# A transformer block on one core: w1 loaded in parts of 6, 4 and 4 blocks, other loads behind pair 1's LayerNorm, and set places for the transposes of pairs 2 and 3

## The chip, the core and the metric

The kernel runs on one core of a Trainium2 chip. The core has a matrix engine (PE, whose weight loads have a row of their own, PEld), a vector engine (DVE), a scalar engine for activations (ACT), a general engine (POOL) and an engine that mainly issues DMAs (SP). Each engine runs its own instruction list in order and waits on semaphores for the others. Sixteen DMA engines move data between the chip's memory (HBM) and the core's on-chip memory. The metric is the device time of one execution, in microseconds (us); lower is better.

## The reference, cut to what matters

The input x is 2048 rows of 448 numbers in bf16. It is normalized once, and two branches read the result; both are added to x.

```python
xn = _layernorm(x, axis=-1)                       # (x - m) / sqrt(v + eps), no gain, no bias
# branch A: linear attention, 16 heads of 28
q, k, v = split(xn @ wqkv)                        # wqkv 448 x 1344
pq = einsum("bhsd,hdf->bhsf", q, w_phi); pk = einsum("bhsd,hdf->bhsf", k, w_phi)
phi_q = concat([softmax(pq), softmax(-pq)]); phi_k = concat([softmax(pk), softmax(-pk)])
kv = einsum("bhsf,bhsd->bhfd", phi_k, v); z = einsum("bhsf->bhf", phi_k)
o = einsum("bhqf,bhfd->bhqd", phi_q, kv) / (einsum("bhqf,bhf->bhq", phi_q, z)[..., None] + 1e-6)
# branch B: feed-forward
h = silu(xn @ w1)                                 # w1 448 x 1792
return x + o @ wo + h @ w2                        # w2 1792 x 448
```

## The kernel before, in words

The 2048 rows are 16 tiles of 128 rows, and two tiles make a pair (pairs 0 to 7). The 1792 columns of w1 are 14 blocks of 128 columns. The 448 rows of w1 are three slabs of 128 rows and a rest of 64 rows, which the kernel calls the tail. PE works with two halves of its rows at once (rows 0 to 63, `UP`, and 64 to 127, `LO`), so that every step is two matmuls of 64 rows side by side.

**Stages.** First the feed-forward branch's first product (FFN1, `xn @ w1`) runs for all pairs, while LayerNorm produces the next pairs. Then come the attention projections with their exponentials, then the attention output and the second product pair by pair. The change touches the FFN1 stage alone, its first 30 us above all.

**Loads (lines 543 to 604).** `load_x(t0, t1)` fetches tiles of x. `load_k` fetches columns of the three full slabs of w1: `w1a` blocks 0 to 3, `w1b` blocks 4 to 7, `w1c` blocks 8 to 13. `load_tail` fetches the 64 tail rows, once for each half (`w1t`, 224 KB each). For pairs 0 and 1 the tail comes instead from small early copies, `w1z`, which `load_z` fetches in a borrowed buffer (`EqT`): blocks 0 to 3 and 4 to 7 on ACT's queue, 8 to 13 on SP's. All other loads are issued by SP, in the order of the program. From `first_loads` on each load is also tied to come after the one before it. Four of these later loads are paced: `for o, d in zip(paced, evp): o.deps.add(d.id)` (line 1136) makes x of tiles 8 to 11, wqk, x of tiles 12 to 15 and wv wait for the ends of the LayerNorm of pairs 1, 2, 3 and 4.

**LayerNorm.** For each tile DVE takes `bn_stats` and `bn_aggr` (lines 608, 610); for each pair it adds eps (`ve`, 616), POOL raises to the power -1/2 (`rstd`, 617), and DVE writes the normalized rows (`xn`, line 624; pairs 0 and 1: line 646). PE transposes them (`xnT_tr`, by `trs`, whose instructions are on line 459) into PSUM banks 6 and 7, and DVE or ACT copies the result to `xnT` (`xnT_ev`; ACT for pair 2, DVE for pairs 3 and up). `lnz_first`, `lnz_second` and `ln_pair(p)` do this for pair 0, pair 1 and the pairs from 2 on.

**FFN1 for pairs 0 and 1.** `ffn1_single(p, f0, f1, i0, i1, bank)` takes the blocks f0 to f1 of one pair: the first half of the range on the upper rows, the second half on the lower, and of these halves the blocks i0 to i1. It makes two groups of steps: in the first group the rows and halves go straight (4 steps for each block pair: three slabs and the tail), in the second crossed (3 steps). A pair is so 49 steps of 256 columns. The calls for one pair are

```python
((0, 4, 0, 2), (4, 8, 0, 2), (8, FT, 0, 2), (8, FT, 2, 3))      # FT = 14
```

Calls are interleaved two by two: first group of u, first group of v, second group of u, second group of v. This is `order0`, and it is an order written out by hand, as order-only ties between PE instructions.

**FFN1 for pairs 2 to 7.** `ffn1_chunk` takes two pairs at once, two blocks at a time; it reads the tail from `w1t`. Between its units lie `fold_tr` (transposes of wqkv in the same banks 6 and 7 that LayerNorm's transposes use) and `fold`.

**The planner.** All other places are chosen by a list scheduler (`schedule`, line 218): it estimates durations and DMA arrivals, and gives each engine the instruction that can start first, with program order deciding between those that are ready within 60 ns. Ties in `odeps` are pure order on one engine; `deps` are real waits. The transposes of pairs 1 to 7 (but not of pair 0) are placed by it, and so is DVE's whole order. What it decides becomes the fixed order of each engine's list, whatever the chip then does.

Of the kernel before, what the change touches and what calls it, by code (L numbers as in the profile page):

```python
# [332 lines left out]
def bass_parallel_sum__linear_kernel_hedgehog__dense_activation_silu__prompt_kernel(  # L333
# [10 lines left out]
    S, D, H, DH, FF = 2048, 448, 16, 28, 1792  # L344
    NT, NPAIR = S // 128, S // 256
    KF = 3
    FT = FF // 128
# [7 lines left out]
    with es:  # L355
# [64 lines left out]
        P = _Prog()  # L420
# [122 lines left out]
        def load_x(t0, t1, eng="sp"):  # L543
            return load(x_sb[:, t0:t1, :], xt[:, t0:t1, :], (t1 - t0) * 128 * D * 2, f"x{t0}", eng)

        def load_k(dst, src, c0, c1, name, eng="sp", o=0):
            return load(dst[:, 0:KF, c0 - o:c1 - o], src[0:384, c0:c1].rearrange("(k p) f -> p k f", p=128),
                        384 * (c1 - c0) * 2, name, eng)

        def load_tail(dst, src, c0, c1, name, eng="sp", eng2="sp", o=0):  # L550
            return [load(dst[r, KF, c0 - o:c1 - o], src[384:448, c0:c1], 64 * (c1 - c0) * 2, name, e)
                    for r, e in ((UP, eng), (LO, eng2))]
# [9 lines left out]
        def load_z(f0, f1, eng):  # L562

            h = (f1 - f0) // 2
            o = w1z_no[0]
            w1z_no[0] += h * 128
            for j in range(2):
                for i in range(h):
                    w1z_at[f0 + j * h + i] = o + 128 * i
            return [load(w1z[r, o:o + h * 128], B_w1[384:448, (f0 + j * h) * 128:(f0 + j * h + h) * 128], 64 * h * 256, "w1z", eng)  # L570
                    for j, r in enumerate((UP, LO))]

        for o in load_z(0, 4, "act") + load_z(4, 8, "act"):
            o.odeps.add(pre_op.id)
        load_x(0, 1)
        load_k(w1_sb, B_w1, 0, 512, "w1a")
        load_x(2, 4)
        load_k(w1_sb, B_w1, 512, 1024, "w1b")
        load_z(8, 14, "sp")
        load_k(w1_sb, B_w1, 1024, FF, "w1c")  # L580
        load_x(4, 6)
        load_x(6, 8)
        load_tail(w1_sb, B_w1, 0, FF, "w1t")
        first_loads = len(P.ops)
        paced = []
        paced.append(load_x(8, 12))
        paced.append(load_k(wraw, A_wqkv, 0, 2 * D, "wqk"))
        load_tail(wraw, A_wqkv, 0, 2 * D, "wqkt")
        phi4 = A_w_phi.rearrange("(g a) d f -> a d g f", a=4)
        for hl in range(2):  # L590
            for r0, a in ((8, 2 + hl), (64, hl)):
                load(BD[r0 + DH * hl:r0 + DH * hl + DH, 0:4, DH * hl:DH * hl + DH], phi4[a], DH * 4 * DH * 2, "phi")
            load(BD[DH * hl:DH * hl + DH, 4, DH * hl:DH * hl + DH], A_w_phi[hl], DH * DH * 2, "phi0")
        paced.append(load_x(12, 16))
        paced.append(load_k(wv_sb, A_wqkv, 2 * D, 3 * D, "wv", "sp", 2 * D))
        load_tail(wv_sb, A_wqkv, 2 * D, 3 * D, "wvt", "sp", "sp", 2 * D)
        w2v = B_w2.rearrange("(f p) d -> p f d", p=128)
# [71 lines left out]
        def lnz_rest():  # L669

            a, b = xnT[LO, 3, 0:2, :], xnT[LO, 7, 0:2, :]
            P.dma(lambda e: e.dma_start(out=a, in_=b), 64 * 512, reads=[b], writes=[a], name="xnTt").odeps.add(paced[3].id)

        def lnz_first():

# [30 lines left out]
        def ln_pair(p, one_by_one=False):  # L706
            t0, t1 = 2 * p, 2 * p + 1
            for t in (t0, t1):
                ln_stats(t)
                if one_by_one:  # L710
                    ln_rstd(t, t + 1)
            if not one_by_one:
                ln_rstd(t0, t1 + 1)
            ln_norm(p, t0)
            ln_norm(p, t1)
            ln_tr(p, [0, 1, 2, 3, 4, 5, 6], 2 if p == NPAIR - 1 else 6, "act" if p in LN_ACT else "dve")
# [7 lines left out]
        def ffn1_chunk(p0, npair, f0, fend, units=(0, 2, 4)):  # L724
            n = npair * 128
            F = 512 // n
            while f0 < fend:
                f1 = min(fend, f0 + F)
                b0 = units[unit_no[0] % len(units)]
                unit_no[0] += 1  # L730
                jobs = []
                for ft in range(f0, f1):
                    jobs.append((lambda r, b: xnT[r, b, p0:p0 + npair, :].rearrange("p a c -> p (a c)"),
                                 lambda r, k, ft=ft: w1_sb[r, k, ft * 128:ft * 128 + 128],
                                 [banks[b0 + par][:, (ft - f0) * n:(ft - f0) * n + n] for par in range(2)],
                                 ft == f0, True))
                units_done.append(contract(jobs, n, True, True, "ffn1_mm"))
                w = f1 - f0
                src = psum[:, b0 * 512:(b0 + 2) * 512].rearrange("p (r c) -> p r c", r=2)[:, :, 0:w * n]
                if w == 1:  # L740
                    dst = hT[:, f0, :, p0:p0 + npair, :].rearrange("p r a c -> p r (a c)")
                else:
                    src = src.rearrange("p r (f c) -> p r f c", f=w)
                    dst = hT[:, f0:f1, :, p0:p0 + npair, :].rearrange("p f r a c -> p r f (a c)")
                o = act(dst, src, ACTF.Silu, "silu", table="silu")
                if exps:
                    o.odeps.update(exps)
                silus.append(o)
                f0 = f1

        def ffn1_single(p, f0, f1, i0, i1, b0, by_tile=False):

            h = (f1 - f0) // 2
            done = [[], []]
            for q, t0, t1 in (((0, 0, 1), (0, 1, 2), (1, 0, 2)) if by_tile else ((0, 0, 2), (1, 0, 2))):
                rr = (UP, LO) if q == 0 else (LO, UP)
                for k in range(KF + 1 - q):
                    for i in range(i0, i1):
                        parts = []
                        for j in range(2):  # L760
                            r, ft = rr[j], f0 + j * h + i
                            xx = xnT[r, k + 4 * t0:k + 4 * t1 - 3:4, p, :]
                            c = (i - i0) * 256 + t0 * 128
                            parts.append((banks[b0 + j][:, c:c + 128 * (t1 - t0)].rearrange("p (t c) -> p t c", c=128),
                                          w1z[r, w1z_at[ft]:w1z_at[ft] + 128] if k == KF else w1_sb[r, k, ft * 128:ft * 128 + 128], xx,
                                          q == 0 and k == 0 and i == i0 and t0 == 0, q == 1 and k == KF - 1))
                        done[q].append(mms(parts, "ffn1_mm", 132.0 / 2 if t1 - t0 == 1 else d_mm(256)))
            for o in done[1]:
                o.syncs.add(done[0][-1].id)
            src = psum[:, b0 * 512:(b0 + 2) * 512].rearrange("p (j f) -> p j f", j=2)[:, :, 0:256 * (i1 - i0)]  # L770
            dst = hT[:, f0:f1, :, p, :].rearrange("p (j i) r c -> p j i r c", j=2)[:, :, i0:i1]
            dst = dst.rearrange("p j i r c -> p j (i r) c")
            src = src.rearrange("p j (a c) -> p j a c", c=128)
            silus.append(act(dst, src, ACTF.Silu, "silu", table="silu"))
            return done
# [40 lines left out]

        ev0, order0 = lnz_first()
        banks_ = iter((0, 2, 4, 0, 2, 4, 0, 2))
        evp, passes = [], []
        for p in range(2):  # L820
            for f0, f1, i0, i1 in ((0, 4, 0, 2), (4, 8, 0, 2), (8, FT, 0, 2), (8, FT, 2, 3)):
                if p == 1 and f0 in (0, 4):
                    k = len(P.ops)
                    ln_pair(2 + f0 // 4)
                    evp.append(P.ops[-1])
                    for o in P.ops[k:]:
                        if o.eng == "dve":
                            o.odeps.add(last1)
                passes.append(ffn1_single(p, f0, f1, i0, i1, next(banks_), f0 == 0 and p == 0))
                if p == 0 and f0 == 0:  # L830
                    k = len(P.ops)
                    evp.append(lnz_second(1))
                    for o in P.ops[k:]:
                        if o.eng == "dve":
                            o.odeps.add(ev0.id)
                    last1 = [o.id for o in P.ops if o.eng == "dve"][-1]
        for u, v in zip(passes[0::2], passes[1::2]):
            order0 += [u[0], v[0], u[1], v[1]]
        for a, c in zip(order0, order0[1:]):
            for o in c:  # L840
                o.odeps.add(a[-1].id)
        ln_pair(4)
        evp.append(P.ops[-1])
        unit_no[0] = 0
        ffn1_chunk(2, 2, 0, 4, (4, 0, 2))
        ln_pair(5)
        for i in range(3):
            ffn1_chunk(2, 2, 4 + 2 * i, 6 + 2 * i, (4, 0, 2))
            fold_tr(3 * i)
# [283 lines left out]
        for a, c in zip(chain, chain[1:]):  # L1133
            for o in c:
                o.odeps.add(a[-1].id)
        for o, d in zip(paced, evp):
            o.deps.add(d.id)
        eks = [o.id for o in P.ops if o.name == "exp_k"]
        for o, d in zip(w2_loads + [wo_load], eks[0::2]):
# [2 lines left out]
        ops = P.ops  # L1142
# [109 lines left out]
```

## Time and profile before

| what | value |
|---|---|
| time of the kernel, median of 3 runs | 157.28 us (157.26 to 157.56) |
| the profiled execution's own time | 158.61 us |
| its span, first to last instruction | 156.8 us |
| PE busy | 149.9 us, 96% of the span |
| PEld, DVE, ACT, POOL busy | 98.0, 99.7, 76.0, 55.0 us |
| granted PE clock | 1.00 throughout |
| bytes moved by DMA | 9.60 MB |

The span is what the profile shows instruction by instruction; the execution's time has some 1.8 us around it. The kernel's chain of waits goes through PE for 80% of the span. A microsecond in which PE stands still early in the kernel is therefore worth looking for, and the rows of PE's weight loads (PEld) show such stops with the name of what ended them.

### The profile page before, as it was taken

To read this page: it belongs to the slowest core of one execution; us is meant where nothing else is said; L and a number is where in the kernel's file an instruction comes from. 1 tells how busy PE (TensorE), PEld (TensorE's weight loads), DVE (VectorE), ACT (ScalarE), POOL (GpSimd) and SP (SyncE) were. 2 spreads that over 40 slices of the span, in tenths; PEclk is the share of its full clock that TensorE was granted. 3 is DMA by queue.
4 is the path that set the end of the run, shared out by engine and by line. 5 is a ranking of instruction groups with operands and counts; after the bars stand their busy time and mean duration, and the time that the engine had idled before them with its cause. 6 is when DMAs were issued, how large, how long until landed. Compare 5 with 4: busy or idle time off the path is not lost.

```text
span 156.8 us, 5661 instructions
## 1 busy us (share of the span) xinstructions
PE 149.9 (96%) x2576; PEld 98.0 (62%) x2576; DVE 99.7 (64%) x177; ACT 76.0 (48%) x89; POOL 55.0 (35%) x79
## 2 busy tenths in 40 slices
PE   6988998999999899999999999999999999999993
PEld 4576886888964445445468887646565655555572
DVE  1948884974236889497696387793846657483203
ACT  3656765558859886986869755220201202021000
POOL 7111111120100677938678023534325160605000
PEclk9999999999999999999999999999999999999999
DMA  4995376000002532040000000001011010101012
GB/s 138 317 281 147 101 212 182 4 4 4 0 4 46 171 112 83 7 117 0 4 0 4 4 0 6 4 0 63 0 59 45 18 63 0 63 2 59 4 63 59
DMA packets 8628, 9.60 MB, mean 61 GB/s; under 512 B 1500, under 2 KB 8220, under 8 KB 8604
## 3 DMA queue, kind: packets, MB, share of 16 engines
q1 hardware_dynamic: 8140, 8.99, 19.3%
q8 instruction: 20, 0.33, 0.9%
q10 hardware_dynamic: 464, 0.25, 0.5%
q14 instruction: 4, 0.03, 0.1%
HBM read 7.37 MB, written 1.84 MB: 59 GB/s over the span
## 4 chain that ended last, share of the span: by engine, by line
PE 80%; DMA 8%; DVE 3%; ACT 3%; SPq 2%; issue 1%; POOL 1%; ACTq 0%
PE psum L446 77%; DMA x_sb<-in_A_x_dram 8%; PE psum L459 3%; SPq L538 2%; ACT EqT L465 1%; DVE st L608 1%; POOL rstd L617 1%; ACT L465 1%; DVE xnT L469 1%; DVE xn_sb L624 1%; ACT scr L465 1%; DVE mv L610 0%; DVE out_sb L1070 0%; DVE ve L616 0%; PE psum L957 0%
## 5 line engine op out<-in xcount | busy, mean ns | idle before, releaser
L446 PE MATMUL psum<-xnT,w_sb 64*128 64x256 bf16 (+1 forms) x768 | 47.4, 268 | 0.7 <-DMA w_sb<-in_B_w_dram 0.5
L446 PE MATMUL psum<-w_sb,hT 64*128 64x448 bf16 (+2 forms) x504 | 46.6, 328 | 0.0
L446 PEld LDWEIGHTS psum<-xnT,w_sb 64*128 64x128 bf16 x768 | 34.6, 94 | 6.6 <-DMA w_sb<-in_B_w_dram 1.0
L465 ACT ACTIVATE hT<-psum 128x1024 bf16<-128x1024 f32 (+1 forms) x29 | 28.3, 994 | 15.0 <-PE psum L446 12.2
L1041 POOL TENSOR_TENSOR xn_sb<-wraw 128x448 bf16<-128x448 f32 (+4 forms) x39 | 20.7, 563 | 36.9 <-DVE wraw L1019 36.9
L446 PEld LDWEIGHTS psum<-w_sb,hT 64*128 64x128 bf16 x504 | 22.7, 94 | 16.5 <-ACT oT L465 0.4
L465 ACT ACTIVATE oT<-psum 128x896 bf16<-128x896 bf16 x8 | 7.3, 917 | 40.4 <-PE psum L459 40.4
L890 POOL TENSOR_TENSOR scr<-scr,Rk 128x1792 bf16<-128x1792 bf16 x6 | 19.3, 3213 | 18.1 <-ACT scr L465 11.4
L465 ACT ACTIVATE EqT<-psum 128x1024 bf16<-128x1024 f32 x16 | 15.5, 1023 | 5.5 <-PE psum L446 5.5
L1019 DVE TENSOR_TENSOR wraw<-psum,Gq 128x1792 f32<-128x1792 f32 (+1 forms) x9 | 16.4, 1818 | 0.9
L446 PE MATMUL psum<-xnT,wqk_sb 64*128 64x512 bf16 x112 | 14.8, 378 | 0.4 <-ACT EqT L465 0.4
L1070 DVE TENSOR_TENSOR out_sb<-psum,x_sb 128x896 bf16<-128x896 f32 (+2 forms) x9 | 8.8, 981 | 9.5 <-PE psum L446 9.4
L1006 DVE RECIPROCAL R<-psum 128x64 f32<-128x64 f32 (+1 forms) x9 | 4.6, 512 | 14.9 <-PE psum L446 14.9
L446 PE MATMUL psum<-wv_sb,xnT 64*128 64x448 bf16 x112 | 14.0, 349 | 0.0
L617 POOL TENSOR_TENSOR rstd<-ve,neghalf 128x2 f32<-128x2 f32 (+1 forms) x8 | 5.4, 672 | 23.8 <-DVE ve L616 23.8
L608 DVE BATCH_NORM_STATS2 st<-x_sb 128x6 f32<-128x448 bf16 x16 | 9.8, 613 | 5.9 <-DMA x_sb<-in_A_x_dram 5.9
L446 PE MATMUL psum<-wo_sb,oT 64*128 64x448 bf16 (+2 forms) x126 | 13.6, 328 | 0.0
L446 PE MATMUL psum<-wqk_sb,xnT 64*128 64x448 bf16 x112 | 13.2, 349 | 0.0
L882 DVE TENSOR_REDUCE Sk<-scr 128x64 f32<-128x1792 bf16 x6 | 12.1, 2013 | 0.6 <-ACT scr L465 0.6
L469 DVE CAST scr<-psum 128x896 bf16<-128x896 f32 x6 | 6.5, 1084 | 9.1 <-PE psum L446 9.1
L465 ACT ACTIVATE scr<-psum 128x896 bf16<-128x896 f32 x12 | 10.4, 921 | 0.7 <-PE psum L446 0.4
L446 PEld LDWEIGHTS psum<-xnT,wqk_sb 64*128 64x128 bf16 x112 | 4.7, 94 | 6.9 <-PE psum L446 1.7
(69 smaller groups left out, 138.7 us busy)
## 6 DMA issues: line engine op xcount, KB each, us to landing
out_dram<-out_sb SPq DMA_DIRECT2D x7, 224.0 KB, 1.9
w_sb<-in_B_w_dram SPq DMA_DIRECT2D x3, 448.0 KB, 3.3
x_sb<-in_A_x_dram SPq DMA_DIRECT2D x2, 448.0 KB, 4.4
w_sb<-in_B_w_dram SPq DMA_DIRECT2D x2, 384.0 KB, 5.0
x_sb<-in_A_x_dram SPq DMA_DIRECT2D x3, 224.0 KB, 7.0
w_sb<-in_B_w_dram SPq DMA_DIRECT2D x3, 224.0 KB, 7.5
wraw<-in_A_wqkv_dram SPq DMA_DIRECT2D x1, 672.0 KB, 4.5
w_sb<-in_B_w_dram SPq DMA_DIRECT2D x1, 576.0 KB, 6.6
```

Source lines behind the costliest of these rows:

```text
L446: r = e.matmul(dst, lhsT, rhs, start=start, stop=stop, skip_group_check=True)
L459: out = e.transpose(dst, src, ident[r, 64:128] if r == LO else ident[r, 0:64])
L465: return P.op("act", d_act(_cols(src)), lambda e: e.activation(dst, src, func, scale=scale), reads=[src], writes=[dst], table=table, name= ...
L469: return P.op("dve", dur, lambda e: e.tensor_copy(dst, src), reads=[src], writes=[dst], name=name)
L608: P.op("dve", 600, lambda e: e.bn_stats(st6[:, t, :], x_sb[:, t, :]), reads=[x_sb[:, t, :]], writes=[st6[:, t, :]], name="bnst")
L617: P.op("pool", 580, lambda e: e.tensor_tensor(r2, v2, nh, ALU.pow), reads=[v2, nh], writes=[r2], name="rstd")
L882: P.op("dve", d_dve(896 * n), lambda e, S4=S4, E4=E4: e.tensor_reduce(S4, E4, AXL.X, ALU.add), reads=[E4], writes=[S3], name="Sk")
L890: lambda e, E5=E5, R5=R5: e.tensor_tensor(E5, E5, R5, ALU.mult),
L1006: P.op("dve", d_rec(32 * n), lambda e, R3=R3, U=U: e.reciprocal(R3, U[:, :, :, DH + 1]), reads=[U[:, :, :, DH + 1]], writes=[r2], name="R2")
L1019: P.op("dve", d_dve(896 * n), lambda e, dsto=dsto, U=U, G3=G3, n=n: e.tensor_tensor(dsto, U[:, :, :, 0:DH], G3[:, :, :, None].broadcast_to ...
L1041: lambda e, dst=dst, a0=a0, a1=a1: e.tensor_tensor(dst, a0, a1, ALU.add),
L1070: P.op("dve", d_dve(2 * (c1 - c0)), lambda e: e.tensor_tensor(dst, ob, xs, ALU.add), reads=[ob, xs], writes=[dst], name="out_ev")
```

## The change

What it does, part by part:

- w1's three loads become 6, 4 and 4 blocks instead of 4, 4 and 6; the early tails follow (`load_z(0, 6)` and `(6, 10)` on ACT's queue, `(10, 14)` on SP's, now behind `w1c`).
- The tail for pairs 2 to 7, `w1t`, leaves the first loads: it now waits for the end of pair 1's LayerNorm, where x of tiles 8 to 11 waited. Right behind it, with no wait of their own, come x of tiles 8 to 11 and of tiles 12 to 15. wqk still waits for pair 2, wv for pair 4.
- FFN1 of pairs 0 and 1 runs as blocks 0 to 5 in two calls, then 6 to 9, then 10 to 13. The interleaving by twos is the same.
- The transposes of pairs 2 and 3 get set places in `order0`: pair 2's ahead of the call for blocks 6 to 9 of pair 1, pair 3's between the first and the second groups of that call and the last.
- DVE's work for pair 4 (all but the statistics of tile 8) and for pair 5 is ordered behind pair 3's copy out of PSUM.

```diff
-        for o in load_z(0, 4, "act") + load_z(4, 8, "act"):
+        for o in load_z(0, 6, "act") + load_z(6, 10, "act"):
             o.odeps.add(pre_op.id)
         load_x(0, 1)
-        load_k(w1_sb, B_w1, 0, 512, "w1a")
+        load_k(w1_sb, B_w1, 0, 768, "w1a")
         load_x(2, 4)
-        load_k(w1_sb, B_w1, 512, 1024, "w1b")
-        load_z(8, 14, "sp")
-        load_k(w1_sb, B_w1, 1024, FF, "w1c")
+        load_k(w1_sb, B_w1, 768, 1280, "w1b")
+        load_k(w1_sb, B_w1, 1280, FF, "w1c")
+        load_z(10, 14, "sp")
         load_x(4, 6)
         load_x(6, 8)
-        load_tail(w1_sb, B_w1, 0, FF, "w1t")
         first_loads = len(P.ops)
-        paced = []
-        paced.append(load_x(8, 12))
+        paced = [load_tail(w1_sb, B_w1, 0, FF, "w1t")[0]]
+        load_x(8, 12)
+        load_x(12, 16)
         paced.append(load_k(wraw, A_wqkv, 0, 2 * D, "wqk"))
...
-        paced.append(load_x(12, 16))
         paced.append(load_k(wv_sb, A_wqkv, 2 * D, 3 * D, "wv", "sp", 2 * D))
...
-        evp, passes = [], []
+        evp, passes, ln_late = [], [], []
         for p in range(2):
-            for f0, f1, i0, i1 in ((0, 4, 0, 2), (4, 8, 0, 2), (8, FT, 0, 2), (8, FT, 2, 3)):
-                if p == 1 and f0 in (0, 4):
+            for f0, f1, i0, i1 in ((0, 6, 0, 2), (0, 6, 2, 3), (6, 10, 0, 2), (10, FT, 0, 2)):
+                if p == 1 and i0 == 0 and f0 < 10:
                     k = len(P.ops)
-                    ln_pair(2 + f0 // 4)
+                    ln_pair(2 + f0 // 6)
                     evp.append(P.ops[-1])
+                    ln_late.append(P.ops[k:])
...
+        early_dve = evp[2].id
         for u, v in zip(passes[0::2], passes[1::2]):
             order0 += [u[0], v[0], u[1], v[1]]
+        tr2, tr3 = ([o for o in ops if o.name == "xnT_tr"] for ops in ln_late)
+        n = len(order0)
+        order0[n - 2:] = [tr3, order0[n - 2], order0[n - 1]]
+        order0.insert(n - 4, tr2)
         for a, c in zip(order0, order0[1:]):
             for o in c:
                 o.odeps.add(a[-1].id)
+        k = len(P.ops)
         ln_pair(4)
+        later4 = [o for o in P.ops[k:] if o.eng == "dve"][2:]
         evp.append(P.ops[-1])
         unit_no[0] = 0
         ffn1_chunk(2, 2, 0, 4, (4, 0, 2))
+        k = len(P.ops)
         ln_pair(5)
+        for o in later4 + [o for o in P.ops[k:] if o.eng == "dve"]:
+            o.odeps.add(early_dve)
...
-        for o, d in zip(paced, evp):
+        for o, d in zip(paced, [evp[0], evp[1], evp[3]]):
             o.deps.add(d.id)
```

More of the change, by code (lines that the diff above doesn't have):

```diff
@@ L671, in lnz_rest @@
             a, b = xnT[LO, 3, 0:2, :], xnT[LO, 7, 0:2, :]
-            P.dma(lambda e: e.dma_start(out=a, in_=b), 64 * 512, reads=[b], writes=[a], name="xnTt").odeps.add(paced[3].id)
+            P.dma(lambda e: e.dma_start(out=a, in_=b), 64 * 512, reads=[b], writes=[a], name="xnTt").odeps.add(paced[2].id)
         def lnz_first():
@@ L828, in bass_parallel_sum__linear_kernel_hedgehog__dense_activation_silu__prompt_kernel @@
                             o.odeps.add(last1)
-                passes.append(ffn1_single(p, f0, f1, i0, i1, next(banks_), f0 == 0 and p == 0))
-                if p == 0 and f0 == 0:
+                passes.append(ffn1_single(p, f0, f1, i0, i1, next(banks_), f0 + p + i0 == 0))
+                if p + f0 + i0 == 0:
                     k = len(P.ops)
```

## The prediction

> **What bounds the kernel now.** I read the profile's page first, then the timeline of PE's weight loads for the stops, then DVE's timeline and the landings of single DMAs for what is behind each stop.
>
> ```profile
> PE 149.9 (96%) x2576; PEld 98.0 (62%) x2576; DVE 99.7 (64%) x177; ACT 76.0 (48%) x89; POOL 55.0 (35%) x79
> PE   6988998999999899999999999999999999999993
> DMA  4995376000002532040000000001011010101012
> ```
>
> PE is full nearly everywhere; before the end only slices 1, 3, 4 and 7 (of 3.9 us each) have less than 9 tenths. DMA is full in slices 2 and 3, has room in 4 and 5 (11.8 to 19.6 us), and is busy again in 6 and 7. The timeline of PE's weight loads names the stops (start, length, and in brackets the idle time before it):
>
> ```profile
> 8.41 0.55 PEld L446 LDWEIGHTS psum<-xnT,w_sb 64*128 64x128 bf16 x12 [0.72 <-DMA w_sb<-in_B_w_dram]
> ...
> 10.89 0.10 PEld L446 LDWEIGHTS psum<-xnT,w_sb 64*128 64x128 bf16 x2 [0.28 <-DMA w_sb<-in_B_w_dram]
> ...
> 14.99 0.31 PEld L459 LDWEIGHTS psum<-ident,xn_sb 64*128 64x128 bf16 x8 [0.93 <-DVE xn_sb L624]
> ...
> 16.10 1.84 PEld L446 LDWEIGHTS psum<-xnT,w_sb 64*128 64x128 bf16 x34
> ...
> 27.66 0.45 PEld L459 LDWEIGHTS psum<-ident,wraw 64*128 64x128 bf16 x24 [1.04 <-DVE xnT L469]
> ```
>
> Four stops, 2.97 us together: w1b late, w1c late, pair 2's LayerNorm late, and banks 6 and 7 not free because pair 5's copy is late. The row without a stop gives the price of a step: 34 loads are 17 steps in 1.84 us, 0.108 us each. DVE's timeline says why the last two stops are there:
>
> ```profile
> 11.96 0.63 DVE L608 BATCH_NORM_STATS2 st<-x_sb 128x6 f32<-128x448 bf16 x1 [1.20 <-DMA x_sb<-in_A_x_dram]
> ...
> 14.55 0.89 DVE L624 TENSOR_SCALAR xn_sb<-x_sb,mv,rstd 128x448 bf16<-128x448 bf16 x3
> ...
> 17.20 0.89 DVE L624 TENSOR_SCALAR xn_sb<-x_sb,mv,rstd 128x448 bf16<-128x448 bf16 x3 [0.28 <-POOL rstd L617]
> ...
> 26.45 0.63 DVE L608 BATCH_NORM_STATS2 st<-x_sb 128x6 f32<-128x448 bf16 x1 [1.40 <-DMA x_sb<-in_A_x_dram]
> 27.00 0.60 DVE L469 COPY xnT<-psum 128x896 bf16<-128x896 bf16 x1
> ```
>
> Tile 4 lands at 11.9 and pair 2 is normalized from 14.55, pair 3 from 17.20. At 26.45 the statistics of tile 12 wait for x, and pair 5's copy, ready since its transposes ended at 25.6, stands behind them in DVE's order. The chain of waits holds that same DMA:
>
> ```profile
> 21.24 5.19 DMA x_sb<-in_A_x_dram
> ```
>
> Landings, each as issue plus time to landing: w1a 1.24+3.8 = 5.0, x of tiles 2 and 3 1.71+4.5 = 6.2, w1b 2.23+6.1 = 8.3, w1c 4.28+6.6 = 10.9, tiles 4 and 5 4.92+7.0 = 11.9, tiles 8 to 11 12.00+3.7 = 15.7. Between w1a's landing and w1c's some 1376 KB land in 5.8 us: 237 KB per us. The windows' 320 to 380 KB per us are what is moved; landings lag, as the last of the DMA engines counts.
>
> **The change, part by part.**
>
> *First part of 6 blocks.* 576 KB instead of 384: it lands 192/237 = 0.8 us later, at 5.8. The first FFN1 step is at 6.53, behind ACT's copy of xnT, so 0.7 us cover it; beyond that each us costs one. x of tiles 2 and 3 slips to 6.9, and pair 1's statistics (6.20 before) have no cover: its normalization moves from 8.09 to 8.75. By the planner's rule the transposes of tile 2 come behind the first call's second group, which is now 10 steps behind the half-width ones that end at 7.70, not 14: PE is there at 8.78 and they end at about 9.5, when both parts of tile 2 are written. New stop: 0.6. Then 3+8 steps and tile 3's transposes follow to 10.8. w1b's new part lands at 9.0 and is needed at 9.8; w1c lands without the 64 KB of tails now behind it, at 10.6, and is needed at 10.8. Both stops go (1.00), against 0.6: gain 0.4. Bounds: 1.0 if x is no later (its landing is interleaved with ACT's queue), -0.3 if w1c lands at 11.2.
>
> The Trainium skill, page "DMA: Bandwidth & Descriptors", section Bandwidth, gives about 358 GB/s as the core's limit from HBM. By it w1's last part would land near 8 us (an estimate from that page), the late w1 would be no bound, the early gain would be 1.0 and the whole sum 1.74 (155.5), toward the better case below. The windows reach that rate from 8 to 10 us, but w1c's landing at 10.9 disagrees, so the sum keeps 0.4.
>
> *Set place for pair 2.* 41 steps lie between 10.8 and it: 15.2. As many bytes are ahead of tile 4 as before, so pair 2 is written from 14.55 to 15.44; the last three transposes wait until then, a stop of 0.2 where 0.93 stood. Gain 0.7.
>
> *Set place for pair 3.* 16 steps on, PE is there at 17.4. DVE and POOL make pair 3 behind pair 2 and write it from 17.20 to 18.09; the transposes then end at 18.25 instead of 17.6: a new stop of 0.65. Before, the planner had FFN1 steps between those transposes. Count as a check: at 18.25 the new order has 78 steps and both sets done; before, 81 steps and both sets were done at 18.93. 18.25+3x0.108 = 18.57, so the three parts together give 0.36 to 0.45; I take 0.4. Ends: -0.3 (another 0.7 at pair 3, below) and 1.2 (DVE's chain earlier by as much as PE's).
>
> *Loads behind pair 1.* SP's wait stands where x of tiles 8 to 11 had it, issued at 12.00. Queued behind it: two tails, two x, wqk, phi, wv. The tail lands where those tiles did, 15.7; its first reader is the chunk of pairs 2 and 3 at 19.5. Tiles 8 to 11 land 448 KB later, 1.4 to 1.9 us at 320 to 237 KB per us: 17.1 to 17.6, or 0.6 sooner if pair 1's end is. Tiles 12 to 15 land at 18.5 to 19.5, seven us ahead of 26.45. That stop goes: gain 1.04. wqk is issued behind pair 2 as before (16.84); at worst it lands at 22.5, its transposes start at 27.66. wv and the small xnT copy slip with pair 4 by about 0.7, from landings near 28; first use past 44. POOL's queue keeps its order.
>
> *Pairs 4 and 5 behind pair 3's copy.* Tile 9's statistics (18.11 before, ahead of that copy) now follow it: 0.65 later for pairs 4 and 5. The planner knows this tie and moves their transposes down PE's list, but on the chip loads are later than it thinks. Ends 0 and 0.65; I take 0.25, nearer to 0 because the timeline of before has no stop over 0.2 at these pairs' transposes. The chunk's own start at 19.5 meets pair 3's copy at 19.0 to 19.6: 0.05.
>
> *Sum.* 0.4 + 1.04 - 0.25 - 0.05 = 1.14. Against the profiled execution, 158.61, that is 157.5; it ran 1.33 above the median of the runs shown, so the forecast on their scale is 157.28 - 1.14 = 156.1.
>
> **Rivals.**
>
> *Better:* x of tiles 2 to 7 lands sooner, the queue being lighter behind it, and pair 3's stop goes with the early one: 0.65+0.6 more, near 154.9. For it: tails no longer compete. Against: they were behind x in the same queue.
>
> *Taken back:* pair 5's copy, 0.65 later, keeps PE waiting at wqk's transposes, and only the early 0.4 is left: 156.9. For it: banks 6 and 7 are shared. Against: before, 1.4 us lie between the end of pair 5's transposes (25.6) and the copy (27.00), more than the delay.
>
> *Slower:* the statistics of tile 8 stand ahead of pair 3's normalization in DVE's order (so they did before, 16.30 against 17.20), and now wait for x behind 448 KB more. Every us that tiles 8 to 11 land after 16.3 moves pair 3, its transposes at their set place and pairs 4 and 5. At 17.5 it costs 1.2 and eats the gain; from there on the kernel is slower, and at 18.0, with tiles 12 to 15 sharing the engines, it is 0.5 slower: 157.8. Against: the planner also sees that x later, and pair 3 may pass first.
>
> **How the numbers follow.** 0.2%, 0.31 us, is about what a measurement of this kernel can tell from no change. Forecast 0.50 (155.5 to 156.7); better 0.15; taken back 0.15, of which a third within 0.31 us; no net change by gains and new stops of one size 0.05; slower 0.15. Faster is 0.50+0.15+0.10 = 0.75, same 0.10, slower 0.15. The range leaves out half of the slower case and a third of the better one: 155.0 to 157.6.
>
> **What would show it.** Right: no stop named DMA at w1's loads near 8.4 and 10.9; one of about 0.6 at the transposes near 8.8; stops at both set places, the second the longer; tile 12's statistics without a wait; no stop of 1 us near 27. Wrong: a wait of DVE for x near 17 ahead of pair 3, wqk's transposes still waiting for DVE's copy, or a first FFN1 step that waits for w1.

## The result

The changed kernel takes 156.01 us (median of 19 runs, 155.54 to 157.14), the kernel before 157.26 us (median of 19, 156.11 to 158.4). The ratio is 0.9927, with a 95% interval of 0.9902 to 0.9953: faster by 0.7%, 1.25 us. The forecast was 156.1 us.

The profile shows a larger step, 156.8 to 154.3 us of span. The profiled execution of the changed kernel took 156.01 us, its median, while that of the kernel before took 158.61, 1.35 above its median. So about half of the 2.5 us belongs to the change, and the stops read from that one profile of before were probably more than a usual execution has. A second profile, below, supports it.

The page of the changed kernel has PE full from slice 2 through slice 12, where slices 3, 4 and 7 had gaps before; DMA is idle in slices 8 to 12, as it was before:

```profile
PE 149.6 (97%) x2576; PEld 98.9 (64%) x2576; DVE 99.6 (65%) x177; ACT 75.7 (49%) x89; POOL 55.0 (36%) x79
...
PE   6999999999998999999999999999999999999992
...
DMA  4967754000004331210000000001101010101012
```

The timeline of PE's weight loads of the changed kernel (start, length, idle before it in brackets) names no stop over 0.2 us between 7.57 us and the projections:

```profile
7.57 0.34 PEld L446 LDWEIGHTS psum<-xnT,w_sb 64*128 64x128 bf16 x12 [0.25 <-ACT xnT L465]
...
9.01 0.27 PEld L459 LDWEIGHTS psum<-ident,EqT 64*128 64x128 bf16 x8
...
10.44 0.64 PEld L446 LDWEIGHTS psum<-xnT,w_sb 64*128 64x128 bf16 x12
...
14.92 0.35 PEld L459 LDWEIGHTS psum<-ident,xn_sb 64*128 64x128 bf16 x14
...
16.87 0.49 PEld L459 LDWEIGHTS psum<-ident,xn_sb 64*128 64x128 bf16 x14
17.29 3.64 PEld L446 LDWEIGHTS psum<-xnT,w_sb 64*128 64x128 bf16 x68
...
26.11 0.50 PEld L459 LDWEIGHTS psum<-ident,wraw 64*128 64x128 bf16 x24
```

At 9.01 are the transposes of tile 2, at 10.44 w1's third part begins, at 14.92 and 16.87 stand the set places of pairs 2 and 3, at 26.11 the first transposes of wqk. None of them waits. DVE's timeline says why (its line numbers are one lower than before):

```profile
11.03 0.63 DVE L607 BATCH_NORM_STATS2 st<-x_sb 128x6 f32<-128x448 bf16 x1 [0.90 <-DMA x_sb<-in_A_x_dram]
...
13.62 0.89 DVE L623 TENSOR_SCALAR xn_sb<-x_sb,mv,rstd 128x448 bf16<-128x448 bf16 x3
...
16.27 0.89 DVE L623 TENSOR_SCALAR xn_sb<-x_sb,mv,rstd 128x448 bf16<-128x448 bf16 x3 [0.81 <-POOL rstd L616]
17.08 0.62 DVE L607 BATCH_NORM_STATS2 st<-x_sb 128x6 f32<-128x448 bf16 x1
17.62 0.61 DVE L469 COPY xnT<-psum 128x896 bf16<-128x896 bf16 x1
```

Tile 4 lands at 11.0 instead of 11.9, pair 2 is normalized from 13.62 instead of 14.55, pair 3 from 16.27 instead of 17.20. The statistics of tile 8 (17.08) follow pair 3's normalization in the list, and in this execution their tiles had landed at 16.7 (issue 12.66 plus 4.0).

### The profile page after: what moved, and what is told of

It is laid out like the page before. It is cut to its first block, busy times and chain, and to the rows that moved or that the text cites. A ratio compares the mean times of both kernels' runs of the same rounds, so it can differ in the third digit from the quotient of the medians.

```text
span 154.3 us, 5662 instructions
## 1 busy us (share of the span) xinstructions
PE 149.6 (97%) x2576; PEld 98.9 (64%) x2576; DVE 99.6 (65%) x177; ACT 75.7 (49%) x89; POOL 55.0 (36%) x79
## 4 chain that ended last, share of the span: by engine, by line
PE 94%; ACT 3%; issue 1%; POOL 0%; DVE 0%; ACTq 0%; POOLq 0%
PE psum L446 90%; PE psum L459 3%; ACT EqT L465 1%; ACT L465 1%; ACT scr L465 1%; ACT xnT L465 0%; DVE out_sb L1080 0%; POOL ident L501 0%; PE psum L967 0%; POOL ones_bf L500 0%; POOL neghalf L504 0%; ACTq L1202 0%; POOLq L1247 0%; POOL ones L505 0%
## 5 line engine op out<-in xcount | busy, mean ns | idle before, releaser
L446 PE MATMUL psum<-xnT,w_sb 64*128 64x256 bf16 (+1 forms) x768 | 46.8, 268 | 0.1
L446 PEld LDWEIGHTS psum<-xnT,w_sb 64*128 64x128 bf16 x768 | 35.3, 94 | 5.2 <-PE psum L446 0.7
L446 PE MATMUL psum<-xnT,wqk_sb 64*128 64x512 bf16 x112 | 14.8, 378 | 0.4 <-ACT EqT L465 0.4
L892 DVE TENSOR_REDUCE Sk<-scr 128x64 f32<-128x1792 bf16 x6 | 12.1, 2013 | 0.6 <-ACT scr L465 0.6
```

Of the source, the lines that this page charges most:

```text
L446: r = e.matmul(dst, lhsT, rhs, start=start, stop=stop, skip_group_check=True)
L892: P.op("dve", d_dve(896 * n), lambda e, S4=S4, E4=E4: e.tensor_reduce(S4, E4, AXL.X, ALU.add), reads=[E4], writes=[S3], name="Sk")
```

## The experiments

Every kernel was timed in rounds with the kernel before on the same chip, but for the first, which is a profile alone. The ratio is to the kernel before, with its 95% interval in brackets; two kernels whose intervals overlap are not told apart by their ratios alone. As a measure that all profiles share I use the time from the first FFN1 weight load to the first weight load of the projections, the FFN1 stretch: 37.6 us in the first profile of before (6.53 to 44.09), 34.9 in the changed kernel (6.71 to 41.58). In all fourteen profiles the execution's own time less this stretch is 121.0 to 121.1 us. So whatever differs between the kernels, or between executions of one of them, lies in this stretch.

**The kernel before, once more.** No edit.

> The kernel before, unchanged, profiled once more. The first profile of it ran 1.3 us above its median, the profile of the changed kernel ran at its median, and the two spans differ by 2.5 us where the medians differ by 1.25. If the four stops of PE are the same in every execution, this span is 156.8 +- 0.3 with stops near 0.72, 0.28, 0.93 and 1.04 us. If landings differ from one execution to the next, the span is 155.3 to 156.3 and the stops together are 1.5 to 2.5 us instead of 2.97.

The span was 156.0 us, the execution 157.73, the FFN1 stretch 36.8. Its stops, by the same view:

```profile
11.37 0.10 PEld L446 LDWEIGHTS psum<-xnT,w_sb 64*128 64x128 bf16 x2 [1.31 <-DMA w_sb<-in_B_w_dram]
...
15.18 0.31 PEld L459 LDWEIGHTS psum<-ident,xn_sb 64*128 64x128 bf16 x8 [0.64 <-DVE xn_sb L624]
...
21.16 0.47 PEld L446 LDWEIGHTS psum<-xnT,w_sb 64*128 64x128 bf16 x10 [0.20 <-ACT hT L465]
```

w1's stops are one of 1.31 instead of 0.72 and 0.28, pair 2's is 0.64 instead of 0.93, and the one near 27, 1.04 us in the first profile, is not there. DVE's rows tell its end:

```profile
25.40 0.63 DVE L608 BATCH_NORM_STATS2 st<-x_sb 128x6 f32<-128x448 bf16 x1
25.94 0.61 DVE L469 COPY xnT<-psum 128x896 bf16<-128x896 bf16 x1
```

Tile 12 was there 1.05 us sooner, so pair 5's copy began at 25.94 instead of 27.00. The largest single stop I had read is not there in every execution of the kernel.

**The later loads alone.** The kernel before with the tails and x of tiles 8 to 15 behind pair 1:

```diff
-        load_tail(w1_sb, B_w1, 0, FF, "w1t")
         first_loads = len(P.ops)
-        paced = []
-        paced.append(load_x(8, 12))
+        paced = [load_tail(w1_sb, B_w1, 0, FF, "w1t")[0]]
+        load_x(8, 12)
+        load_x(12, 16)
...
-        paced.append(load_x(12, 16))
```

> The kernel before with the order of the later loads alone: the tails of w1 wait for pair 1's LayerNorm, x of tiles 8 to 15 right behind them. w1 in 4, 4 and 6 blocks, no set places, no ties for pairs 4 and 5. Theory A (the stops add up, tile 4 lands when it did): only the stop near 27 goes, 0.8 to 1.0 us, ratio 0.994 +- 0.002; statistics of tile 4 start near 11.9 and the stop ahead of pair 2's transposes stays at 0.7 to 1.0. Theory B (x of tiles 4 to 7 lands sooner because the tails no longer follow it in the queue): statistics of tile 4 start near 11.0, the stop ahead of pair 2's transposes is under 0.3, ratio 0.988 to 0.992.

Ratio 1.0002 (0.9972 to 1.0032): nothing, where theory A wanted 0.6%. Tile 4 landed at 11.1, and the stop ahead of pair 2's transposes was 0.42, between the two theories. PE's rows and DVE's:

```profile
10.55 0.10 PEld L446 LDWEIGHTS psum<-xnT,w_sb 64*128 64x128 bf16 x2 [0.69 <-DMA w_sb<-in_B_w_dram]
...
14.15 0.31 PEld L459 LDWEIGHTS psum<-ident,xn_sb 64*128 64x128 bf16 x8 [0.42 <-DVE xn_sb L623]
...
19.72 0.91 PEld L446 LDWEIGHTS psum<-xnT,w_sb 64*128 64x128 bf16 x18 [0.67 <-issue]
```

```profile
18.45 0.63 DVE L607 BATCH_NORM_STATS2 st<-x_sb 128x6 f32<-128x448 bf16 x1 [1.20 <-DMA x_sb<-in_A_x_dram]
18.99 0.61 DVE L469 COPY xnT<-psum 128x896 bf16<-128x896 bf16 x1
```

The stop near 27 is gone, and a new one of 0.67 stands at 19.72, where the chunk of pairs 2 and 3 begins: its input is pair 3's copy at 18.99, and that copy stands in DVE's list behind the statistics of tile 8, which waited 1.20 us for x. Those tiles now queue behind 448 KB of tails. (The view calls the releaser "issue"; that the copy is the cause is read from the two times.) This is the mechanism of my slower rival, at pair 3's copy instead of its normalization.

**The parts of w1 alone.** The kernel before with parts, calls and early tails of 6, 4 and 4 blocks, and nothing else of the change.

```diff
-        load_k(w1_sb, B_w1, 0, 512, "w1a")
+        load_k(w1_sb, B_w1, 0, 768, "w1a")
...
-            for f0, f1, i0, i1 in ((0, 4, 0, 2), (4, 8, 0, 2), (8, FT, 0, 2), (8, FT, 2, 3)):
+            for f0, f1, i0, i1 in ((0, 6, 0, 2), (0, 6, 2, 3), (6, 10, 0, 2), (10, FT, 0, 2)):
```

> The kernel before with w1 in parts of 6, 4 and 4 blocks alone, its tails with them; the later loads as before, no set places, no ties. Theory A: the two stops at w1 go (1.0) against a new one at tile 2's transposes of 0 to 0.6, the stops ahead of pair 2's transposes and near 27 stay: ratio 0.994 to 0.999. Theory B: the same at w1; tile 4 still lands near 11.9, since the tails follow it. Third way C (the new parts by themselves bring x sooner): tile 4's statistics start near 11.0 here too.

Ratio 0.9982 (0.9952 to 1.0012), unresolved alone. In its profile no row names a DMA of w1 any more and nothing waits at tile 2's transposes; pair 2's transposes, which the planner puts early, wait 0.52 us at 13.73 for the normalization. Tile 4 landed at 10.7, as the third way said, with the tails behind it. The stop near 27, which theory A kept, is not there: tile 12 landed at 24.3, and the wqk transposes began at 25.55 without a wait.

**The change without the parts.** The complement: loads, set places and ties kept, w1 in 4, 4 and 6 blocks.

```diff
-        load_k(w1_sb, B_w1, 0, 768, "w1a")
+        load_k(w1_sb, B_w1, 0, 512, "w1a")
...
-            for f0, f1, i0, i1 in ((0, 6, 0, 2), (0, 6, 2, 3), (6, 10, 0, 2), (10, FT, 0, 2)):
+            for f0, f1, i0, i1 in ((0, 4, 0, 2), (4, 8, 0, 2), (8, FT, 0, 2), (8, FT, 2, 3)):
```

> The changed kernel with w1 back in parts of 4, 4 and 6 blocks (calls and early tails with them); loads behind pair 1, set places and ties stay. Theory P (the parts are most of the gain): a stop of 0.3 to 1.4 us ahead of w1's third part near 11, ratio 0.996 to 1.000. Theory Q (places and loads are most of it): ratio 0.992 to 0.995. Tile 4 landed at 11.1 to 12.1 in three profiles with 4, 4 and 6 blocks, at 10.1 to 11.0 in seven with 6, 4 and 4: if the parts cause that, 11.0 to 12.1 here; if it is chance, 10.1 to 11.0 as often.

Ratio 0.9985 (0.9952 to 1.0019): without the parts 0.6% of the 0.7% is missing, near 0.9 us. Theory P holds in size, but not in place: in the profiled execution the only stop for w1 was 0.34 us, at the second part:

```profile
8.20 0.55 PEld L446 LDWEIGHTS psum<-xnT,w_sb 64*128 64x128 bf16 x12 [0.34 <-DMA w_sb<-in_B_w_dram]
```

Tile 4 landed at 10.8, inside the range of the kernels with 6, 4 and 4 blocks, so this run speaks for chance in the last sentence above. The edit is also not the parts alone, since the set places are counted in calls: with the old calls pair 2's stands 7 steps later, pair 3's 3 steps, and some of the 0.9 us may be theirs.

**The change without the set places.** The planner places the transposes of pairs 2 and 3.

```diff
-        order0[n - 2:] = [tr3, order0[n - 2], order0[n - 1]]
-        order0.insert(n - 4, tr2)
```

> The changed kernel without the set places: the planner places the transposes of pairs 2 and 3. It puts them earlier in PE's list, pair 2's behind some 42 to 47 steps instead of 62. Normalization of pair 2 starts at 13.6 as in the changed kernel. Theory A (set places matter): PE reaches pair 2's transposes near 13 and stands 0.5 to 0.9 us; ratio against before 0.995 to 0.998, 0.3 to 0.6 us slower than the changed kernel. Rival (landings and loads are all of it): no stop over 0.3, ratio 0.992 +- 0.002 as the changed kernel.

Ratio 0.9949 (0.9922 to 0.9977), 0.2% above the change's, but the intervals overlap, and the median, 156.23 us, lies between the two that the changed kernel has (156.01, and 156.29 below). A cost of the missing places is not shown here. The rival's "no stop" failed, and so did my place for it: pair 2's transposes did not wait, since tile 4 landed at 10.2; the stop is at pair 4's:

```profile
21.26 0.31 PEld L459 LDWEIGHTS psum<-ident,xn_sb 64*128 64x128 bf16 x8 [0.57 <-DVE xn_sb L623]
```

Tile 8's statistics had waited 0.74 us for x, until 18.23, and everything of pair 4 behind them.

**Which loads matter: tails first, tiles 12 to 15 late, both.** Three edits of the changed kernel. First the tails back among the first loads:

```diff
+        load_tail(w1_sb, B_w1, 0, FF, "w1t")
         first_loads = len(P.ops)
-        paced = [load_tail(w1_sb, B_w1, 0, FF, "w1t")[0]]
-        load_x(8, 12)
+        paced = [load_x(8, 12)]
         load_x(12, 16)
```

> The changed kernel with the tails of w1 back among the first loads, behind x of tiles 6 and 7, as in the kernel before; x of tiles 8 to 11 wait for pair 1 and tiles 12 to 15 follow. Theory B (tails behind x slow x down): statistics of tile 4 start near 11.9, pair 2 and 3 are late at their set places, 0.5 to 1.0 us slower than the changed kernel (ratio 0.996 to 1.000 against before). Theory D (landing of x just differs from one execution to the next, 10.3 to 12.1 in the six profiles so far, whatever lies behind it): ratio as the changed kernel's, 0.992 +- 0.002, and tile 8's statistics start 1 to 1.5 us sooner, near 16 to 17.

Ratio 0.9919 (0.9882 to 0.9956), tile 4 at 10.1: with these parts the tails behind x do not slow x, and theory B falls. Tile 8's statistics began at 14.7, sooner than theory D said too. Second, x of tiles 12 to 15 back behind wqk and phi, waiting for pair 3:

```diff
-        load_x(12, 16)
         paced.append(load_k(wraw, A_wqkv, 0, 2 * D, "wqk"))
...
+        paced.append(load_x(12, 16))
         paced.append(load_k(wv_sb, A_wqkv, 2 * D, 3 * D, "wv", "sp", 2 * D))
```

> The changed kernel with x of tiles 12 to 15 back where they were: behind wqk and phi, waiting for pair 3. Theory A of the prediction (the stop near 27 was worth 1.04 us): it comes back, 0.7 to 1.0 us slower than the changed kernel, ratio against before 0.997 to 1.000. Theory D (that stop is there only in executions in which those tiles land after 26; in the second profile of before they landed at 25.4 and there was none): within 0.3 us of the changed kernel, ratio 0.991 to 0.995, tile 12's statistics near 24 to 25.5.

Ratio 0.9928 (0.9902 to 0.9955), the changed kernel's own, so theory A falls. Tile 12's statistics waited until 25.68, and the stop behind them was 0.22 us. Third, both edits together, which is the old order of all later loads:

> The changed kernel with all later loads as before: the tails among the first loads, tiles 8 to 11 behind pair 1, 12 to 15 behind pair 3. Kept are the parts of 6, 4 and 4 blocks, the set places, the ties of pairs 4 and 5. Theory A (loads are worth 1.04): ratio 0.998 to 1.002. Theory D (the parts and the places are all of it): ratio 0.992 +- 0.002, within 0.3 us of the changed kernel.

Ratio 0.9963 (0.9936 to 0.9989), 0.4% above the change's. The medians on this chip are closer, 156.51 us against 156.29 for the changed kernel and 156.01 for the second edit, so the old loads cost some 0.2 to 0.6 us. Theory D, which made the loads worth nothing, looks wrong as well, though 0.2 us would lie within its bound. Here the stop near 27 is back, 0.64 us:

```profile
27.66 0.41 PEld L459 LDWEIGHTS psum<-ident,wraw 64*128 64x128 bf16 x24 [0.64 <-DVE scr L469]
```

DVE's copies of wqk's first transposes stood behind tile 12's statistics, which waited 0.86 us for x, until 26.05. In the second edit the same copies stand behind the same statistics; there tile 12 landed at 25.66 instead of 26.03. The kernel with the parts alone, with the old order of these loads too, had no such stop when tile 12 landed at 24.3. So the stop follows tile 12's landing in the execution at hand, and one profile of each kernel can't say how much of that is the order of the loads.

**The tails first, without the set places.** The first of these three edits together with the removal above.

> The changed kernel with the tails among the first loads and without the set places, so the planner places the transposes of pairs 2 and 3. In the kernel without places and with late tails, PE stood at pair 4's transposes, not at pair 2's. Theory A (set places are needed): ratio 0.995 to 0.998, 0.4 us or more slower than the kernel with tails first, with a stop of over 0.3 at pair 2's or 3's transposes. Theory E (set places only undo what tiles 8 to 11 landing late costs): ratio 0.992 +- 0.002, no stop over 0.3.

Ratio 0.9956 (0.9928 to 0.9985), 0.3 to 0.4% slower than with places. The ratios' intervals overlap, but the kernel with places ran again on the same chip (below), and there the means of the runs differ by some 0.5 us, with a 95% interval of 0.15 to 0.77. So the places matter where tile 8 is early (14.8 in this profile), as theory A said of the time. Its stops are elsewhere, both ahead of FFN1 steps:

```profile
14.22 0.09 PEld L446 LDWEIGHTS psum<-xnT,w_sb 64*128 64x128 bf16 x1 [0.38 <-issue]
...
16.54 0.22 PEld L446 LDWEIGHTS psum<-xnT,w_sb 64*128 64x128 bf16 x6 [0.26 <-ACT hT L465]
```

The view puts the second down to ACT, which reads FFN1's results out of PSUM (hT); just ahead of the first, which it calls "issue", ACT ended two such instructions at 14.14.

**The changed kernel, and the one with tails first, once more.**

> The changed kernel once more, on the same chip as the three others, with a second profile. Ratio 0.992 +- 0.003. If landings are what differs between executions, tile 4's statistics start anywhere from 10.3 to 12.1, and where tiles 8 to 11 land after 18 a stop of about 0.5 stands at pair 4's transposes near 21; the first profile of it had neither.

Ratio 0.9923 (0.9892 to 0.9953). This profile (FFN1 stretch 35.3) has a stop that the first lacked, not at pair 4's transposes but two us sooner, where the chunk of pairs 2 and 3 begins; tiles 8 to 11 landed at 17.7 (12.37 plus 5.4):

```profile
18.96 2.32 PEld L446 LDWEIGHTS psum<-xnT,w_sb 64*128 64x128 bf16 x44 [0.56 <-DVE xnT L469]
```

```profile
17.76 0.63 DVE L607 BATCH_NORM_STATS2 st<-x_sb 128x6 f32<-128x448 bf16 x1 [0.70 <-DMA x_sb<-in_A_x_dram]
18.30 0.61 DVE L469 COPY xnT<-psum 128x896 bf16<-128x896 bf16 x1
```

> The changed kernel with the tails among the first loads, once more. If it is really a little better than the changed kernel: median 155.9 +- 0.2, ratio 0.990 to 0.993, few runs above 156.5. If the first measurement was chance: ratio 0.992 to 0.995 and runs up to 157 as the changed kernel has.

Ratio 0.9924 (0.9897 to 0.9950), median 156.12 (155.82 to 156.55). With tails first the medians are 155.93 and 156.12 against 156.01 and 156.29 for the changed kernel. They can't be told apart; the highest runs, 156.65 and 156.55 (of 7 and 8) against 157.14 and 157.05 (of 19 and 12), and two profiles without any stop over 0.2 fit a kernel that lacks the wait at tile 8, no more.

**Only the early tails of blocks 8 to 13 behind w1's third part.** To see why tile 4 lands sooner with the new parts; an edit of the kernel before.

```diff
-        load_z(8, 14, "sp")
         load_k(w1_sb, B_w1, 1024, FF, "w1c")
+        load_z(8, 14, "sp")
```

> The kernel before with one load moved: the early tails of blocks 8 to 13 behind w1's third part instead of ahead of it. If their place is why w1's third part and tile 4 land later with 4, 4 and 6 blocks: third part lands near 9.5 to 10, tile 4 near 10.1 to 11, stop near 11 under 0.1, ratio 0.995 to 0.998. If it is the size of the parts: third part at 10.5 to 11.3, tile 4 at 11.1 to 12.1, ratio 0.998 to 1.002.

Ratio 1.0007 (0.9975 to 1.0040). w1's third part landed at 11.1 and tile 4 at 12.6, the latest of all, so their place alone is not the cause. The stops were no smaller; the second, which this view calls "issue", ended when an early tail (`EqT`) landed, at 10.49:

```profile
8.57 0.55 PEld L446 LDWEIGHTS psum<-xnT,w_sb 64*128 64x128 bf16 x12 [0.85 <-DMA w_sb<-in_B_w_dram]
...
10.60 0.14 PEld L446 LDWEIGHTS psum<-xnT,EqT 64*128 64x128 bf16 x4 [1.48 <-issue]
```

The ties for pairs 4 and 5 were not run alone: without them the planner writes the same list for every engine, so in this kernel they change nothing.

## Why the prediction was right

The total came out within 0.1 us, and that is luck in good part: its terms were wrong in opposite directions. The sum also took stops that were read from an execution 1.33 us above the median off the median itself. Of the five signs named for being right three came true (no stop for w1, tile 12 without a wait, no stop of 1 us near 27, which the second profile of before lacks as well), and two did not (the stop at tile 2's transposes, the stops at the set places).

*First part of 6 blocks* ("x of tiles 2 and 3 slips to 6.9", "new stop: 0.6", gain 0.4). Here the step from the part's landing to x's failed. The part landed at 5.5 (1.24 plus 4.25; said: 5.8) and x of tiles 2 and 3 at 6.4, only 0.2 later than before, so tile 2's normalization moved to 8.31 and its transposes at 9.01 waited for nothing. (Two of the other profiles with 6 blocks have a wait of 0.15 and 0.20 there.) Over all profiles the first part lands at 4.8 on average with 4 blocks and at 5.5 with 6: 192 KB more cost 0.6 us, not 0.8, and x behind it slips by 0.2, not by as much. Both of w1's stops went, as said. With the old parts they were 1.00, 1.31, 0.69, 0.34 and 0.85 us in five profiles, the last without its wait for an early tail, and undoing the parts costs some 0.9 us: within the change the term is near 0.9, not 0.4. Alone the parts gave 0.3, which noise does not tell from 0.

*Set places* (a stop of 0.2 at pair 2's, 0.65 at pair 3's, against 0.93 removed). Both stops are absent, because the premise "as many bytes are ahead of tile 4 as before", and so the same landing, failed: tile 4 landed at 11.0 and 10.9 in the two profiles of the changed kernel. The better rival's picture of pair 3's stop vanishing is what happened, but its reason, the tails behind x, is not borne out: with the new parts tile 4 lands no later when they stand there (10.1 and 10.2). Undoing the places costs some 0.5 us with the tails first; with the tails late no cost is shown.

*Loads behind pair 1* (gain 1.04). Mis-sized. Moving tiles 12 to 15 alone changes nothing (0.9928 without the move), and all the moves undone cost 0.2 to 0.6 us. The stop of 1.04 was that of one execution in which tile 12 landed at 26.4; the second had none. Taking one execution's stop for every execution's was the error. It should also depend on when PE arrives (the later PE is at wqk's transposes, the smaller the stop), but no run varies that alone.

*Pairs 4 and 5 behind pair 3's copy* (0.25 and 0.05 lost). The ties change nothing in the lists, and pair 4's and 5's transposes have no wait over 0.2 us in either profile of the changed kernel. The 0.05 at the chunk's start named the right wait: it was 0 in the first profile and 0.56 us in the second.

*Slower rival.* Its wait is real: DVE's statistics of tile 8 wait for x behind the tails, 0.70 and 1.20 us in two profiles, and PE then stands 0.56 and 0.67. In the changed kernel it does not decide, as the planner put pair 3's normalization ahead of those statistics, as I had argued; it is pair 3's copy that they hold up. In the kernel with the loads alone it stands where the gain should have shown; that the one ate the other is not shown.

*Taken back* did not happen: pair 5's copy began at 25.26, and the wqk transposes at 26.11 without a wait.

The Trainium skill's limit of about 358 GB/s (page "DMA: Bandwidth & Descriptors", section Bandwidth) put w1's last part near 8 us by the estimate made there. It landed at 10.3 (2.80 plus 7.5) in the changed kernel, so this reading of it stays wrong. The one-microsecond windows of the kernel before even show 384 and 392 GB/s (9 to 10 us, 19 to 20 us). That the stops at w1 went is due to PE having six blocks' work first: it needs the second part near 9.5, where it stood waiting from 7.7 before. The third part, needed at 10.44, is in time by 0.2 us only because it also lands sooner, at 10.3 instead of 10.9.

One reading of the profile's page was incomplete: slice 14 (51 to 55 us) has 8 tenths as well. The changed kernel has that too, in slice 13, so it does not bear on the change.

Summed from what was undone, 0.9 for the parts, 0 to 0.5 for the places and 0 to 0.6 for the loads are 0.9 to 2.0, against 1.25 measured; alone, parts and loads gave 0.3 and 0.0, and the places were not run alone. It looks as if the pieces need each other, each stop removed letting PE reach the next late thing, but these differences are too near the noise to show it.

## What to carry to other kernels

Read a stop for the landing behind it, and ask whether that landing would be the same in another execution; a second profile of the kernel before would have removed my largest term. Do not simply add stops along one engine's list: price each for the time at which the engine would arrive once the earlier ones are gone. And when a load is moved behind others, look at what is queued behind its first reader on that reader's engine, not only at who reads the data.

## What was not expected of the hardware

Tile 4, issued at 4.9 to 5.0 in every profile, landed at 10.8 to 12.6 in five profiles with w1 in 4, 4 and 6 blocks (11.9, 12.1, 11.1, 10.8, 12.6) and at 9.8 to 11.0 in nine with 6, 4 and 4 (11.0, 10.7, 10.2, 10.1, 10.1, 10.1, 10.9, 9.8, 10.2), with the same bytes ahead of it. On average that is 11.7 against 10.3, and on each of the two chips that ran both kinds the new parts were sooner (12.1, 11.1 against 10.7, 10.2; and 10.8, 12.6 against 9.8, 10.2). The place of the early tails does not explain it. What is queued behind does not with the new parts; with the old ones the two kernels with late tails have the two earliest landings (11.1, 10.8), so there it is not excluded. The sizes of the runs in w1's three parts were not tried by themselves, so the cause stays open.

Within a kind, tile 4's landings spread by 1.2 to 1.8 us, about as much as the whole effect of the change. Little of that lies between executions of one kernel: the three that were profiled twice repeat (11.9 and 12.1; 11.0 and 10.9; 10.1 and 10.2). Other landings do not repeat so well: tile 12 in the kernel before came at 26.4 and 25.4, tile 8 in the changed kernel at 16.7 and 17.7.

The traces keep the times of the 16 counts that make up each landing, and these say where the spread comes from. Half of tile 4's counts are in by 9.4 to 10.2 in all fourteen profiles, with old and new parts alike. What differs is the last few. In the changed kernel 15 of 16 are in by 9.9 and 9.7, and the last one comes at 11.0 and 10.9; in the other seven profiles with 6, 4 and 4 blocks the last follows the one before it within 0.5 us. In the first profile of before 13 are in by 10.15, and the other three come at 11.8 to 11.9. The same holds for the largest stop of that profile: 15 of tile 12's counts were in by 24.65, and the last came at 26.43, so the 1.04 us near 27 waited for a single count. The Trainium skill, page "DMA: Bandwidth & Descriptors", section "Why a DMA increments its semaphore by 16 and not by 1", says that only the full count of 16 engines means that all data has landed, so the slowest of them sets a landing; these counts agree. Which engine lags, and why, no view here shows.
